# A memory-attention, ReLU² and SoLU chain: the last group's maximum taken by a matmul with ones instead of GpSimd's all-reduce, scales made ahead, and the last tile's output product done in two column halves

## The chip, the core and the metric

The kernel runs on one core of one Trainium2 chip. The metric is the device time of one execution in microseconds, from three timed runs. One further execution was recorded by the hardware profiler, and every time inside the kernel comes from that one.

The engines are named as the profile names them: PE is the matrix engine (PEld its weight loads), DVE the vector engine, ACT the scalar engine, POOL is GpSimd, and SPq and ACTq are the two queues from which the DMAs here are issued. Each engine works its instructions off in the order in which the program lists them for it, and waits for other engines by semaphores.

## The reference

Three stages follow each other. Attention over 32 memory slots per head gives `x` of 4608 tokens by 512. The second stage is a two-layer block with a squared ReLU. The third, with which this change has to do, is this:

```python
def _moe2_ref(x, w_in, w_out, g_ln):
    h = x @ w_in                                   # 4608 x 512 by 512 x 1024
    h_max = np.max(h, axis=-1, keepdims=True)
    e = np.exp(h - h_max)
    sm = e / (np.sum(e, axis=-1, keepdims=True) + 1e-09)
    solu = h * sm
    mu = np.mean(solu, axis=-1, keepdims=True)
    var = np.mean((solu - mu) ** 2, axis=-1, keepdims=True)
    ln = (solu - mu) / np.sqrt(var + 1e-06) * g_ln
    return (ln @ w_out).astype(np.float32)         # by 1024 x 512
```

All inputs and outputs are float32.

## The kernel before

**Precision.** Most products are made from float16 pairs: each factor is scaled by a power of two and split into a high and a low half, and three products (high by high, high by low, low by high) are added up in PSUM. `PASSES` lists the three. So each operand needs a scale before it can be split.

**Scales of x.** The 4608 tokens of the third stage's input fall into four groups of 1152. For each group the kernel finds the largest magnitude: every x tile leaves a column of per-partition maxima, `x_max(g)` reduces these columns on DVE, and `all_max` takes the maximum over the 128 partitions on POOL, in one all-reduce (L182). `x_scale(g)` turns the result into a scale in six tiny DVE instructions; `x_col(p)` gives the column of scales for a pair `p`, and where a pair straddles two groups it adds two more instructions to combine them (L1534).

**Third stage.** It runs over 18 pairs of 128-token tiles (`pair`, L1683). Of each pair, seven block products fill three PSUM banks on PE (`product`, L1610), ACT copies the banks out (L1701, L1709, L1720, L1736) and DVE adds to them (L1681). Then each tile goes through `solu_max`, `solu_exp`, `solu_2`, `solu_3` and `solu_4`: maximum (DVE), exponential (ACT), normalisation (DVE, and on POOL the `rstd` of L1661 and the `so` of L1662), float16 high half (ACT, L1668), low half (DVE, L1673), and a DMA transpose into `lt` (L1675). Two pairs later `gemm4` multiplies the transposed tile by `w_out` in 24 matmuls (L1760), `out4` scales the PSUM bank on ACT (L1774) and sends it to DRAM. Pair `p` also splits the x of pair `p+1` (`split_part`: ACT L1580, DVE L1582), with the scale from `x_col`.

**Order.** The program is recorded in the order in which it is written: `pair` lists the steps by hand and puts the `gemm4` pieces of an earlier pair (`fill`) between the products, so that PE has something to do while ACT and DVE work on the banks. A wait therefore holds everything written behind it for the same engine. The last group's maximum is taken after pair 1; its scale is first needed by pair 13. The scale of group 1, though, is made inside pair 3, when it splits the x of pair 4, which straddles groups 0 and 1. After pair 17 come the last four tiles' products (`rest`) with nothing else left for PE.

Of the kernel before, what the change touches and what calls it, by code (L numbers as in the profile page):

```python
# [8 lines left out]
FP32 = mybir.dt.float32  # L9
FP16 = mybir.dt.float16  # L10
# [56 lines left out]
def tile_mem_attention__moe_relu2__solu_ln(  # L67
# [15 lines left out]
    nc = tc.nc  # L83
# [136 lines left out]

    def mm_max(dg):
        w = dg.shape[1]
        mp = ps_h.tile([128, 2, 512], FP32, tag="h", name="mp")
        nc.tensor.matmul(
            out=mp[:, 0, 0:128 * w], lhsT=pools_b["ones"], rhs=dg.rearrange("p w t -> p (w t)"), start=True, stop=True
        )
        al = pools_b["m"].tile([128, w], FP32, tag=f"mal{w}", name="mal")
        nc.vector.tensor_reduce(
            out=al, in_=mp[:, 0, 0:128 * w].rearrange("p (w t) -> p w t", w=w), op=ALU.max, axis=AX
        )  # L230
        return al

# [1191 lines left out]

    def prep2_open():
        attn_ctx.close()
        for nm, bufs in (("x", 2), ("s", 2), ("o", 2)):
            pools_b[nm] = ctx.enter_context(tc.tile_pool(name=f"pb_{nm}", bufs=bufs))
        w2 = wts.tile([128, 16384], FP16, tag="win", name="w2_t")
        W2["out"] = w2[:, 0:2 * KF2 * DM].rearrange("p (a k f) -> p a k f", a=2, k=KF2)  # L1430
        W2["hi"] = w2[:, 2 * KF2 * DM:2 * KF2 * DM + 14 * 512].rearrange("p (b k f) -> p b k f", b=7, k=2)
        W2["lo"] = [raw_p.tile([128, 7, 512], FP16, tag="raw", name="w2_lo") for k in range(2)]
        for i in range(8):
            tag = ("e2", "nat", "lt", "lt")[i // 2]
            W2[i] = pools_b["s"].tile([128, 2, 512], FP32, tag=tag, name="w2", bufs=4 if tag == "lt" else 2)
# [44 lines left out]
    def prep2(i):  # L1480
        if i == 0:
            w2_sums(0)
            for k in range(2):
                w2_split(k, 0)
                w2_split(k, 1)
        elif i == 1:
            w2_split(0, 2)
            w2_split(0, 3)
            w2_sums(1)
        elif i == 2:  # L1490
            w2_split(1, 2)
            w2_split(1, 3)
            load_x(0)
            load_x(1)
        elif i == 3:
            sums_x(0)
            x_col(0)
        elif i == 5:
            split_part(0, 0)
        elif i == 7:  # L1500
            split_part(0, 1)
            load_x(2)
            sums_x(1)
# [23 lines left out]
    def x_scale(g):  # L1527
        sc = pow2_scale(xal_t.pop(g), xiv[:, g:g + 1])
        nc.vector.tensor_scalar(out=xsc[:, g:g + 1], in0=sc, scalar1=0.25, scalar2=None, op0=ALU.mult)
        nc.vector.tensor_tensor(out=xiv[:, g:g + 1], in0=xiv[:, g:g + 1], in1=iw2, op=ALU.mult)  # L1530

    xcol_t = {}

    def x_col(p):  # L1534


        g0, g1 = p * 256 // GRP, (p * 256 + 255) // GRP
        for g in (g0, g1):
# [104 lines left out]
    def solu_2(p, t):  # L1643
# [19 lines left out]
            out=so, in0=so, scalar1=mv[:, 0:1], scalar2=rstd[:, 0:1], op0=ALU.add, op1=ALU.mult  # L1663
        )

    def solu_3(p, t):
        nat = pools_b["s"].tile([128, 2, DFF2], FP16, tag="nat", name="nat")
        nc.scalar.copy(out=nat[:, 0, :], in_=h_of(p, t))  # L1668
        so_t[p, t] = nat

    def solu_4(p, t):
        nat = so_t.pop((p, t))
        nc.vector.tensor_tensor(out=nat[:, 1, :], in0=h_of(p, t), in1=nat[:, 0, :], op=ALU.subtract)  # L1673
        lt = pools_b["s"].tile([128, 2, KF2, 128], FP16, tag="lt", name="lt", bufs=4)
        nc.sync.dma_start_transpose(  # L1675
            out=lt.rearrange("p a k t -> p (a k) t"), in_=nat.rearrange("p a f -> p (a f)")
        )
        ln_t[2 * p + t] = lt
# [72 lines left out]
    out_v = out.rearrange("(b p c) d -> b c p d", b=NB, c=C)  # L1751

    def gemm4(i, part):
        if part == 0:
            gt["y4", i] = ps_y.tile([128, 512], FP32, tag="y", name="y2")
        lt, y = ln_t[i], gt["y4", i]
        steps = [(f, pl, pw) for f in range(KF2) for pl, pw in PASSES]
        for x in range(6 * part, 6 * part + 6):
            f, pl, pw = steps[x]
            nc.tensor.matmul(  # L1760
                out=y[:, 0:DM],
                lhsT=lt[:, pl, f, :],
                rhs=W2["out"][:, pw, f, :],
                start=(x == 0),
                stop=(x == len(steps) - 1),
            )
        if part == 3:
            ln_t.pop(i)

    def out4(i):  # L1770
        if i < 0:
            return
        o = pools_b["o"].tile([128, DM], FP32, tag="o", name="o")
        nc.scalar.activation(out=o, in_=gt.pop(("y4", i))[:, 0:DM], func=ACTF.Copy, scale=io2[:, 0:1])  # L1774
        for x, (off, n, bb, c, p) in enumerate(runs(i * 128, 128)):
            eng = nc.scalar if i == NTILE - 1 and x else nc.sync
            eng.dma_start(out=out_v[bb, c, p:p + n, :], in_=o[off:off + n, :])

    def tiles4(p):
        return [lambda i=i, part=part: gemm4(i, part) for i in (2 * p, 2 * p + 1) for part in range(4)]  # L1780
# [51 lines left out]
    with tc.manual_schedule():  # L1832
        make_identity(nc, ident)
        nc.vector.memset(ones, 1.0)
        nc.vector.memset(nhalf, -0.5)
        nc.vector.memset(half, 0.5)
        nc.gpsimd.memset(pmx, LOWEST)
        nc.vector.memset(c15, 2.0 ** -15)
        nc.vector.memset(kmT, 0.0)
        nc.vector.memset(ones_f, 1.0)  # L1840

        for step in FIRST.split():
            name, _, at = step.partition(".")
            now[0] = step
            STEPS[name](*(int(a) for a in at))
        now[0] = ""
        nc.gpsimd.dma_start(out=gl, in_=g_ln.rearrange("(k p) -> p k", p=128))

        LAST = NB - 1
        for n in range(1, NB):  # L1850
            for j in range(2):
                if n == 1 and j == 0:
                    w_in_scale()
                    load_q(2, 3)
                    early_load(0)
# [12 lines left out]
                if n % 2 and j and n < LAST:  # L1868
                    x_max(n // 2)
                    xal_t[n // 2] = all_max(xal_t[n // 2], "xal")  # L1870


        pair(0, [lambda d=d, x=x: gemm2_q(LAST, 1, d, x) for d in (1, 2) for x in range(4)])
        pair(1, [lambda x=x: gemm2_q(LAST, 1, 3, x) for x in range(4)], (0, 1, 1, 2))
        x_max(3)
        xal_t[3] = all_max(xal_t[3], "xal")
        for p in range(2, NPAIR):
            pair(p, tiles4(p - 2))
        p = NPAIR - 1
# [46 lines left out]
```

## Time and profile before

| | us |
|---|---|
| median of three runs | 1064.44 (1062.96 to 1064.65) |
| the profiled execution | 1064.40 |
| its span, first to last instruction | 1062.6 |
| busy on PE, of the span | 1031.9 (97%) |
| busy on DVE | 831.4 (78%) |
| busy on ACT | 579.5 (55%) |
| busy on POOL | 232.8 (22%) |

PE is busy nearly all the time, so what matters is the few places where it is not: an instruction of another engine is worth something only where PE waits for it. Matmuls overlap, so in the timeline the busy time of a row is a little more than the row's share of PE's time; the distance between the starts of two equal rows is the better measure. Between two pairs everything repeats, so one pair's period can be compared with the next one's. A row's square brackets give the idle time of its engine just before it and what ended it; "issue" there means that the profile shows nothing that the engine waited for.

### The profile page before, as it was taken

The numbers are of one execution on the slowest core, as the hardware profiler recorded it, in microseconds if no ns is written. First come the engines' busy times: TensorE is split into PE (matmuls) and PEld (weight loads), VectorE is DVE, ScalarE is ACT, GpSimd is POOL, SyncE is SP. The second block draws the span as 40 slices with busy tenths as digits, with TensorE's granted clock in tenths as the row PEclk, the third lists the DMA queues.
The fourth block names the chain that finished last, engine by engine and source line by source line (L and its number), as shares of the span: only waits on it lengthen the run. The fifth ranks groups of instructions, "written<-read, shape, count | busy, mean of one in ns | idle before, by whom it ended". The sixth has DMA issues, their size and how long they took to land.

```text
span 1062.6 us, 21249 instructions
## 1 busy us (share of the span) xinstructions
PE 1031.9 (97%) x8569; PEld 684.2 (64%) x8569; DVE 831.4 (78%) x1548; ACT 579.5 (55%) x869; POOL 232.8 (22%) x237
## 2 busy tenths in 40 slices
PE   5799999999999999999999999999799999999998
PEld 4577777777777777777777777764344444444443
DVE  4889988868768767768768766787888898898872
ACT  3689755653654554563563654753544555545442
POOL 0000200220120120120120134232343353353411
PEclk9999999999999999999999999999899999999999
DMA  9994533733832833833832343123345354354343
GB/s 290 289 271 130 128 109 89 170 104 69 200 102 76 196 99 72 201 98 79 194 97 57 63 147 114 44 60 95 90 106 119 93 128 104 86 136 103 80 90 89
DMA packets 196402, 129.25 MB, mean 122 GB/s; under 512 B 137168, under 2 KB 179408, under 8 KB 196304
## 3 DMA queue, kind: packets, MB, share of 16 engines
q1 hardware_dynamic: 196160, 127.70, 46.7%
q8 instruction: 67, 1.10, 0.5%
q14 instruction: 31, 0.25, 0.1%
q10 hardware_dynamic: 112, 0.20, 0.1%
q0 software_dynamic: 32, 0.00, 0.0%
HBM read 71.83 MB, written 23.07 MB: 89 GB/s over the span
## 4 chain that ended last, share of the span: by engine, by line
PE 87%; DVE 6%; DMA 3%; issue 2%; ACT 1%; SPq 0%; POOL 0%; ACTq 0%; DVEq 0%; POOLq 0%
PE y L1200 32%; PE hp L1118 15%; PE y L1760 15%; PE hb L1610 13%; PE y L1040 2%; PE hp L1012 2%; PE wp L736 2%; DMA q_s<-in_q_dram 2%; PE sp L885 1%; PE kp L526 1%; DMA wt_s<-in_v_dram 1%; DVE hmx L1629 1%; DMA kv_s<-in_v_dram 1%; DVE bs L1654 1%; DVE so L1649 1%
## 5 line engine op out<-in xcount | busy, mean ns | idle before, releaser
L1200 PE MATMUL y<-g,w_out 128*128 128x288 f16 x2688 | 339.6, 286 | 0.0
L1200 PEld LDWEIGHTS <-w_out 128*128 128x128 f16 x2880 | 277.3, 97 | 87.8 <-issue 12.3
L1760 PE MATMUL y<-w_t,lt 128*128 128x512 f16 x864 | 201.0, 381 | 0.5 <-DMA lt<-nat 0.5
L1610 PE MATMUL hb<-w_t,xs 128*128 128x512 f16 x504 | 165.3, 381 | 6.3 <-ACT so L1701 6.3
L1118 PE MATMUL hp<-aT,vwt 128*128 128x288 f16 x1344 | 166.9, 286 | 0.0
L1118 PEld LDWEIGHTS <-vwt 128*128 128x128 f16 x1344 | 131.4, 98 | 33.3 <-issue 0.2
L1760 PEld LDWEIGHTS <-lt 128*128 128x128 f16 x864 | 84.8, 98 | 103.6 <-issue 1.7
L1610 PEld LDWEIGHTS <-xs 128*128 128x128 f16 x756 | 74.3, 98 | 95.0 <-issue 8.4
L1610 PE MATMUL hb<-w_lo,xs 128*128 128x512 f16 x252 | 96.0, 381 | 0.0
L1183 DVE TENSOR_TENSOR g<-r_s,g 128x576 f16<-128x576 f32 x112 | 88.3, 788 | 3.9
L1222 ACT ACTIVATE x<-y,bcol,cs 128x288 f32<-128x288 f32 x60 | 35.2, 586 | 101.1 <-PE y L1200 88.4
L1176 ACT ACTIVATE r_s<-r 128x576 f32<-128x576 f32 x112 | 76.7, 685 | 21.2 <-DVE g L1183 18.2
L1129 ACT ACTIVATE r<-hp 128x576 f32<-128x576 f32 x120 | 77.4, 645 | 13.2 <-PE hp L1118 7.2
L1661 POOL TENSOR_TENSOR rstd<-ve,nhalf 128x1 f32<-128x1 f32 x36 | 35.3, 982 | 215.2 <-DVE mv L1659 208.3
L1101 DVE CAST g<-r_s 128x576 f16<-128x576 f32 x112 | 54.0, 482 | 19.1 <-ACT r_s L1176 19.1
L1668 ACT CAST nat<-so 128x1024 f16<-128x1024 f32 x36 | 37.4, 1040 | 53.9 <-POOL so L1662 53.9
L321 DVE TENSOR_REDUCE xmx<-x 128x1 f32<-128x288 f32 x64 | 28.8, 450 | 47.9 <-ACT x L1222 47.6
L1681 DVE TENSOR_TENSOR so<-hb,so 128x512 f32<-128x512 f32 x54 | 37.2, 689 | 27.4 <-PE hb L1610 27.2
L1673 DVE TENSOR_TENSOR nat<-so,nat 128x1024 f16<-128x1024 f32 x36 | 45.5, 1263 | 9.4 <-ACT nat L1668 9.2
L962 POOL TENSOR_TENSOR e<-e,ssm 96x512 f32<-96x512 f32 x18 | 18.8, 1046 | 153.8 <-DVE ssm L957 121.1
L1638 ACT ACTIVATE e<-so,nm,xiv 128x1024 f32<-128x1024 f32 x36 | 44.7, 1242 | 9.9 <-DVE nm L1631 9.9
L1662 POOL TENSOR_SCALAR so<-so,mv,rstd 128x1024 f32<-128x1024 f32 x36 | 49.0, 1361 | 3.8
(269 smaller groups left out, 1432.5 us busy)
## 6 DMA issues: line engine op xcount, KB each, us to landing
x_d<-x SPq DMA_DIRECT2D x64, 144.0 KB, 2.0
kv_s<-in_k_dram SPq DMA_DIRECT2D x31, 288.0 KB, 8.4
kv_s<-in_v_dram SPq DMA_DIRECT2D x31, 288.0 KB, 9.0
xt<-x_d SPq DMA_DIRECT2D x16, 512.0 KB, 4.3
q_s<-in_q_dram SPq DMA_DIRECT2D x21, 288.0 KB, 5.0
out_dram<-o SPq DMA_DIRECT2D x23, 192.0 KB, 2.3
w_out<-in_moe_w_in_dram SPq DMA_DIRECT2D x4, 1024.0 KB, 15.7
raw<-in_moe_w_out_dram SPq DMA_DIRECT2D x4, 1024.0 KB, 11.9
```

Source lines behind the costliest of these rows:

```text
L1101: nc.vector.tensor_copy(out=g_of(n, j, 0)[:, 2 * fp:2 * fp + 2, 0:BLK], in_=gt["r2", j, fp])
L1118: nc.tensor.matmul(out=hp[:, u, 0:BLK], lhsT=vt[:, pw, R, f * 128:(f + 1) * 128], rhs=aT[:, CJ * j:CJ * (j + 1), pa, R, :], start=(x == 0) ...
L1129: nc.scalar.activation(out=r, in_=gt.pop(("h", j, fp))[:, :, 0:BLK], func=ACTF.Relu, scale=scale)
L1176: nc.scalar.activation(out=r2, in_=r, func=ACTF.Square)
L1183: (nc.vector if eng == "D" else nc.gpsimd).tensor_tensor(out=g_of(n, j, 1)[:, fs, 0:BLK], in0=gt.pop(("r2", j, fp)), in1=g_of(n, j, 0)[:, ...
L1200: nc.tensor.matmul(out=y[:, 0:w], lhsT=w_out_t[d][:, pw, f, :], rhs=g_of(n, j, pg)[:, f, 0:w], start=(x == 0), stop=(x == len(steps) - 1),)
L1610: nc.tensor.matmul(out=hp_t[p][bank], lhsT=xs[:, px, a, kk, :], rhs=W2["lo"][kk][:, b, :] if pw else W2["hi"][:, b, kk, :], start=first an ...
L1638: nc.scalar.activation(out=e, in_=h_of(p, t), func=ACTF.Exp, scale=iv[:, 0:1], bias=nm[:, 0:1], accum_out=sm)
L1662: nc.gpsimd.tensor_scalar(out=so, in0=so, scalar1=mv[:, 0:1], scalar2=rstd[:, 0:1], op0=ALU.add, op1=ALU.mult)
L1668: nc.scalar.copy(out=nat[:, 0, :], in_=h_of(p, t))
L1673: nc.vector.tensor_tensor(out=nat[:, 1, :], in0=h_of(p, t), in1=nat[:, 0, :], op=ALU.subtract)
L1760: nc.tensor.matmul(out=y[:, 0:DM], lhsT=lt[:, pl, f, :], rhs=W2["out"][:, pw, f, :], start=(x == 0), stop=(x == len(steps) - 1),)
```

## The change

1. The maximum of the last group (group 3) is taken otherwise. `mm_max_put` puts the per-partition maxima on the diagonal of a 128 by 128 tile (one DVE instruction, after pair 1); at the head of pair 4 `mm_max` multiplies it by a tile of ones on PE into a PSUM bank of the tag `h2`, and DVE reduces the bank. The tile of ones is set by POOL when the third stage's pools are opened. The three earlier groups keep the all-reduce.
2. `x_col` remembers its results, and the columns of pairs 0, 4, 5 and 9 are made together at the time when only that of pair 0 was made; the column of pair 13 is made right after `mm_max`.
3. At the end, `solu_3` and `solu_4` of tile 34 are written before `solu_2` of tile 35; those of tile 35 stand two pieces of `rest` later than before, behind `out4` of tile 32; tile 35's transpose is issued in two parts, high half and low half.
4. Tile 35's product runs in two halves of 256 columns, 24 matmuls each, the high-half passes first in each; `out4` evicts and stores each half by itself.

```diff
     def mm_max(dg):
         w = dg.shape[1]
-        mp = ps_h.tile([128, 2, 512], FP32, tag="h", name="mp")
+        mp = pools_b["h"].tile([128, 512], FP32, tag="h2", name="mp")
...
+        pools_b["ones"] = pools_b["m"].tile([128, 128], FP32, tag="ones", name="ones_m")
+        nc.gpsimd.memset(pools_b["ones"], 1.0)
...
             sums_x(0)
-            x_col(0)
+            for p in (0, 4, 5, 9):
+                x_col(p)
...
+    def solu_T(p, t, a):
+        nat, lt = so_t[p, t], ln_t[2 * p + t]
+        nc.sync.dma_start_transpose(
+            out=lt[:, a].rearrange("p a k t -> p (a k) t"), in_=nat[:, a].rearrange("p a f -> p (a f)")
+        )
...
         lt, y = ln_t[i], gt["y4", i]
-        steps = [(f, pl, pw) for f in range(KF2) for pl, pw in PASSES]
-        for x in range(6 * part, 6 * part + 6):
-            f, pl, pw = steps[x]
+        w = DM // halves
+        order = [(f, ps) for f in range(KF2) for ps in PASSES]
+        if i == NTILE - 1:
+            order.sort(key=lambda s: s[1][0])
+        steps = [(h, f, pl, pw) for h in range(halves) for f, (pl, pw) in order]
+        for h, f, pl, pw in steps[6 * halves * part:6 * halves * (part + 1)]:
             nc.tensor.matmul(
-                out=y[:, 0:DM],
+                out=y[:, h * w:(h + 1) * w],
                 lhsT=lt[:, pl, f, :],
-                rhs=W2["out"][:, pw, f, :],
...
         x_max(3)
-        xal_t[3] = all_max(xal_t[3], "xal")
+        xal_t[3] = mm_max_put(xal_t[3])
         for p in range(2, NPAIR):
+            if p == 4:
+                xal_t[3] = mm_max(xal_t[3])
+                x_col(13)
             pair(p, tiles4(p - 2))
...
         solu_max(p, 1)
         out4(2 * p - 3)
+        solu_3(p, 0)
         solu_exp(p, 1)
+        solu_4(p, 0)
         solu_2(p, 1)
-        solu_3(p, 0)
-        solu_4(p, 0)
         for x, f in enumerate(rest):
             f()
-            if x == 2:
+            if x == 4:
                 solu_3(p, 1)
                 solu_4(p, 1)
-            if x % 4 == 3:
+            if x == 13:
+                out4(2 * p + 1, 0)
+            elif x == 15:
+                out4(2 * p + 1, 1)
+            elif x % 4 == 3:
                 out4(2 * p - 2 + x // 4)
```

On POOL, at the end of pair 1 and in pair 2, the kernel before has these rows (`al` is the all-reduced maximum, `rstd` and `so` the two steps of the normalisation; L1661 and L1662 are lines before the change):

```order
L1662 TENSOR_SCALAR so<-so,mv,rstd 128x1024
L184 ISA
L184 ISA al<-xmax 128x1
L1661 ISA
L1661 TENSOR_TENSOR rstd<-ve,nhalf 128x1
L1662 TENSOR_SCALAR so<-so,mv,rstd 128x1024
```

and the changed kernel, at the same place, these:

```order
L1667 TENSOR_SCALAR so<-so,mv,rstd 128x1024
L1666 TENSOR_TENSOR rstd<-ve,nhalf 128x1
L1667 TENSOR_SCALAR so<-so,mv,rstd 128x1024
L1568 TENSOR_TENSOR xm<-xt 128x256
L1568 TENSOR_TENSOR xm<-xm,xt 128x256
```

The all-reduce is gone, and with it an ISA row ahead of it and another ahead of the `rstd` that follows.

On DVE, inside pair 3, the kernel before makes the scale of group 1 between the maximum `hmx` of a tile and the split `xs` of pair 4:

```order
L1631 TENSOR_SCALAR nm<-hmx,xiv 128x1
L238 TENSOR_SCALAR pm_9449<-al 128x1
L240 TENSOR_SCALAR ex<-pm_9449 128x1
L244 TENSOR_SCALAR sc<-ex 128x1
L247 TENSOR_SCALAR xiv<-ex 128x1
L1529 TENSOR_SCALAR xsc<-sc 128x1
L1530 TENSOR_TENSOR xiv<-xiv,iw_112 128x1
L1545 TENSOR_TENSOR xsc<-xsc 128x1
L1545 TENSOR_TENSOR xiv<-xiv 128x1
L1582 SCALAR_TENSOR_TENSOR xs<-xm,xsc,xs 128x1024
```

In the changed kernel that place has no such rows, and the head of pair 4 has these on DVE, with the reduction of PE's bank `mp` first:

```order
L1664 TENSOR_SCALAR mv<-mv 128x1
L228 TENSOR_REDUCE mal<-mp 128x1
L238 TENSOR_SCALAR pm_9631<-mal 128x1
L240 TENSOR_SCALAR ex<-pm_9631 128x1
L244 TENSOR_SCALAR sc<-ex 128x1
L247 TENSOR_SCALAR xiv<-ex 128x1
L1532 TENSOR_SCALAR xsc<-sc 128x1
L1533 TENSOR_TENSOR xiv<-xiv,iw_112 128x1
L1550 TENSOR_TENSOR xsc<-xsc 128x1
L1550 TENSOR_TENSOR xiv<-xiv 128x1
L1634 TENSOR_REDUCE hmx<-so 128x1
```

So the eight scale instructions leave the stretch in front of pair 4's split and stand, for another group, in front of a `hmx` one pair later.

On PE, in the changed kernel, the two halves of the last tile meet here (`y` is the PSUM bank, `lt` the transposed tile, `w_t` holds w_out; the wait is for ACT):

```order
L1779 LDWEIGHTS lt
L1779 MATMUL y_12236<-w_t,lt 128x256
L1779 LDWEIGHTS lt
L1779 MATMUL y_12236<-w_t,lt 128x256 [waits Activation_49]
L1779 LDWEIGHTS lt
L1779 MATMUL y_12236<-w_t,lt 128x256
```

The fourth row is the second half's first matmul: it waits until ACT has evicted the first half. The kernel before has 24 matmuls of 512 columns there and no wait among them.

## Rows read from the trace of the kernel before

**Rows 1.** Waits of PE over the span: who for whom, total, times, longest.

```profile
PE hb L1610 <- ACT so L1701: 6.3, 1, 6.3
...
PE y L1760 <- DMA lt<-nat: 0.5, 1, 0.5
```

**Rows 2.** Busy time by stretch: length, PE, PEld, DVE, ACT, POOL, PE clock.

```profile
750.00:760.00 10.00, 10.00 (x38) 4.11 (x37) 9.27 (x17) 5.99 (x11) 5.73 (x6) 0.78 0.46 104
```

**Rows 3.** Timeline of all engines, pairs 2 and 3: start, busy, engine, line.

```profile
720.66 2.75 PE L1760 MATMUL y<-w_t,lt 128*128 128x512 f16 x12
...
728.29 0.56 POOL L184 PARTITION_ALL_REDUCE al<-xmax  x1 [6.07 <-DVE mv L1659]
...
735.73 0.59 POOL L1661 TENSOR_TENSOR rstd<-ve,nhalf 128x1 f32<-128x1 f32 x1 [6.88 <-issue]
...
738.74 1.47 DVE L1673 TENSOR_TENSOR nat<-so,nat 128x1024 f16<-128x1024 f32 x1 [6.37 <-ACT nat L1668]
...
740.08 2.75 PE L1760 MATMUL y<-w_t,lt 128*128 128x512 f16 x12
...
745.93 0.14 DVE L238 TENSOR_SCALAR pm<-al 128x1 f32<-128x1 f32 x1
...
746.74 0.15 DVE L1545 TENSOR_TENSOR xiv<-xiv 128x1 f32<-128x1 f32 x1
746.92 1.15 ACT L1580 ACTIVATE xs<-xm,xsc 128x1024 f16<-128x1024 f32 x1 [5.93 <-DVE xiv L1545]
...
748.54 0.57 ACT L1701 COPY so<-hb 128x512 f32<-128x512 f32 x1
...
749.17 0.59 PE L1610 MATMUL hb<-w_t,xs 128*128 128x512 f16 x1 [6.33 <-ACT so L1701]
```

**Rows 4.** Timeline of all engines in pair 5, an undisturbed one.

```profile
788.01 2.75 PE L1760 MATMUL y<-w_t,lt 128*128 128x512 f16 x12
...
788.33 0.58 ACT L1709 COPY so<-hb 128x512 f32<-128x512 f32 x1
...
793.19 0.38 PE L1610 MATMUL hb<-w_t,xs 128*128 128x512 f16 x1
```

**Rows 5.** Timeline of DVE after the scale of group 0.

```profile
664.02 0.45 DVE L321 TENSOR_REDUCE xmx<-x 128x1 f32<-128x288 f32 x1 [4.49 <-ACT x L1222]
```

**Rows 6.** Timeline of POOL where the third stage's pools are opened.

```profile
632.91 1.76 POOL L1460 TENSOR_TENSOR w2s<-w 128x512 f32<-128x512 f32 x1 [8.97 <-DMA w<-w_d]
```

**Rows 7.** Line L204, six ones-by-diagonal products: ns min/median/max, first and last start.

```profile
L204 PEld LDWEIGHTS mp<-first x12: 186/191/338, 21.3 to 121.4; 128*128 128x128 f32 x12
L204 PE MATMUL mp<-first x12: 272/275/579, 21.3 to 121.5; 128*128 128x128 f32 x12
```

**Rows 8.** Line L209, the reduction of such a bank.

```profile
L209 DVE TENSOR_REDUCE first<-mp x6: 277/282/292, 28.0 to 122.0; 128x1 f32<-128x128 f32 x6
```

**Rows 9.** Line L173, nine float16 matmuls of 256 columns in a row.

```profile
L173 PE MATMUL ta<-first x9: 272/273/283, 42.7 to 43.6; 128*128 128x256 f16 x9
```

**Rows 10.** Timeline of all engines at the end.

```profile
1035.36 11.82 PE L1760 MATMUL y<-w_t,lt 128*128 128x512 f16 x54
...
1042.71 1.22 DVE L1673 TENSOR_TENSOR nat<-so,nat 128x1024 f16<-128x1024 f32 x1
...
1047.66 10.53 PE L1760 MATMUL y<-w_t,lt 128*128 128x512 f16 x48 [0.49 <-DMA lt<-nat]
...
1058.29 0.69 ACT L1774 ACTIVATE o<-y,io 128x512 f32<-128x512 f32 x1 [4.49 <-PE y L1760]
1059.00 0.39 ACTq L1777 DMA_DIRECT2D out_dram<-o  x1
```

**Rows 11.** Groups of ACT by shape: busy, mean ns of one.

```profile
L1580 ACT ACTIVATE xs<-xt,xsc 128x256 f16<-128x256 f32 x18 | 9.0, 500 | 0.0
```

**Rows 12.** DMA issues in the last 33 us: KB, median us to landing.

```profile
out_dram<-o SPq DMA_DIRECT2D x4, 64.0 KB, 2.2
out_dram<-o ACTq DMA_DIRECT2D x1, 192.0 KB, 2.6
```

More of the change, by code (lines that the diff above doesn't have):

```diff
@@ L222, in mm_max @@
         w = dg.shape[1]
-        mp = ps_h.tile([128, 2, 512], FP32, tag="h", name="mp")
+        mp = pools_b["h"].tile([128, 512], FP32, tag="h2", name="mp")
         nc.tensor.matmul(
-            out=mp[:, 0, 0:128 * w], lhsT=pools_b["ones"], rhs=dg.rearrange("p w t -> p (w t)"), start=True, stop=True
+            out=mp[:, 0:128 * w], lhsT=pools_b["ones"], rhs=dg.rearrange("p w t -> p (w t)"), start=True, stop=True
         )
@@ L228, in mm_max @@
         nc.vector.tensor_reduce(
-            out=al, in_=mp[:, 0, 0:128 * w].rearrange("p (w t) -> p w t", w=w), op=ALU.max, axis=AX
+            out=al, in_=mp[:, 0:128 * w].rearrange("p (w t) -> p w t", w=w), op=ALU.max, axis=AX
         )
@@ L1426, in prep2_open @@
         attn_ctx.close()
-        for nm, bufs in (("x", 2), ("s", 2), ("o", 2)):
+        for nm, bufs in (("x", 2), ("s", 2), ("o", 2), ("m", 1)):
             pools_b[nm] = ctx.enter_context(tc.tile_pool(name=f"pb_{nm}", bufs=bufs))
@@ L1530, in x_scale @@
         nc.vector.tensor_tensor(out=xiv[:, g:g + 1], in0=xiv[:, g:g + 1], in1=iw2, op=ALU.mult)
-    xcol_t = {}
+    col_t = {}
     def x_col(p):
+        if p in col_t:
+            return col_t[p]
         g0, g1 = p * 256 // GRP, (p * 256 + 255) // GRP
@@ L1540, in x_col @@
                 x_scale(g)
+        c = col_t[p] = g0 if g0 == g1 else NT // GRP + g0 // 2
         if g0 == g1:
-            return g0
-        c = NT // GRP + g0 // 2
+            return c
         for t, op in ((xsc, ALU.min), (xiv, ALU.max)):
@@ L1669, in solu_3 @@
         so_t[p, t] = nat
+        if 2 * p + t == NTILE - 1:
+            ln_t[2 * p + t] = pools_b["s"].tile([128, 2, KF2, 128], FP16, tag="lt", name="lt", bufs=4)
+            solu_T(p, t, slice(0, 1))
     def solu_4(p, t):
-        nat = so_t.pop((p, t))
+        nat = so_t[p, t]
         nc.vector.tensor_tensor(out=nat[:, 1, :], in0=h_of(p, t), in1=nat[:, 0, :], op=ALU.subtract)
[L1674 to L1678, printed above, removed]
+        if 2 * p + t == NTILE - 1:
+            solu_T(p, t, slice(1, 2))
+        else:
+            ln_t[2 * p + t] = pools_b["s"].tile([128, 2, KF2, 128], FP16, tag="lt", name="lt", bufs=4)
+            solu_T(p, t, slice(0, 2))
+        so_t.pop((p, t))
     def h_add(out_, bank):
@@ L1753, in gemm4 @@
     def gemm4(i, part):
+        halves = 2 if i == NTILE - 1 else 1
         if part == 0:
@@ L1756, in gemm4 @@
         lt, y = ln_t[i], gt["y4", i]
-        steps = [(f, pl, pw) for f in range(KF2) for pl, pw in PASSES]
-        for x in range(6 * part, 6 * part + 6):
-            f, pl, pw = steps[x]
+        w = DM // halves
[4 more added lines that the diff above has]
+        for h, f, pl, pw in steps[6 * halves * part:6 * halves * (part + 1)]:
             nc.tensor.matmul(
-                out=y[:, 0:DM],
+                out=y[:, h * w:(h + 1) * w],
                 lhsT=lt[:, pl, f, :],
-                rhs=W2["out"][:, pw, f, :],
-                start=(x == 0),
-                stop=(x == len(steps) - 1),
+                rhs=W2["out"][:, pw, f, h * w:(h + 1) * w],
+                start=(f == 0 and (pl, pw) == PASSES[0]),
+                stop=(f == KF2 - 1 and (pl, pw) == PASSES[-1]),
             )
@@ L1768, in gemm4, with out4 @@
             ln_t.pop(i)
-    def out4(i):
+    def out4(i, half=None):
         if i < 0:
             return
-        o = pools_b["o"].tile([128, DM], FP32, tag="o", name="o")
-        nc.scalar.activation(out=o, in_=gt.pop(("y4", i))[:, 0:DM], func=ACTF.Copy, scale=io2[:, 0:1])
+        cs = slice(0, DM) if half is None else slice(half * DM // 2, (half + 1) * DM // 2)
+        if not half:
+            gt["o", i] = pools_b["o"].tile([128, DM], FP32, tag="o", name="o")
+        o = gt["o", i]
+        nc.scalar.activation(out=o[:, cs], in_=gt["y4", i][:, cs], func=ACTF.Copy, scale=io2[:, 0:1])
         for x, (off, n, bb, c, p) in enumerate(runs(i * 128, 128)):
-            eng = nc.scalar if i == NTILE - 1 and x else nc.sync
-            eng.dma_start(out=out_v[bb, c, p:p + n, :], in_=o[off:off + n, :])
+            eng = nc.scalar if half and x else nc.sync
+            eng.dma_start(out=out_v[bb, c, p:p + n, cs], in_=o[off:off + n, cs])
     def tiles4(p):
```

## The prediction

> **What bounds the kernel now.** I read the waits of PE first, since PE is the engine that is nearly always busy. From the third stage on there are two entries: one wait of 6.3 us for ACT's copy L1701, and one of 0.5 us for a transpose [rows 1]. The reader is to see that nothing else holds PE there, so the change can be worth something at two places only. The second view is the timeline around the long wait. PE's twelve `gemm4` matmuls at the head of a pair start at 720.66 in pair 2 and at 740.08 in pair 3, a period of 19.42 us [rows 3]. In pair 5 they start at 788.01 [rows 4]. Two periods would have taken 38.84 us; 47.93 us went by, so the long wait costs 788.01 − 740.08 − 38.84 = 9.09 us. That is more than 6.33 us: in the stretch after it PE's granted clock averages 0.78 [rows 2], that is, part of it at 1.2 GHz and the rest at 2.4 GHz, after PE had stood idle. So about 2.8 us of the 9.09 are matmuls at half pace.
>
> Read backwards, the wait is a chain [rows 3]. PE starts at 749.17, when ACT's copy (748.54 plus 0.57) is done. ACT is in order, and ahead of the copy stands the split `xs` of pair 4, held for 5.93 us by the last of eight scale instructions on DVE. DVE is in order too, and had been held for 6.37 us by an ACT cast, which needs `so` from POOL. POOL's `rstd` started at 735.73 after 6.88 us in which it waited for nothing shown; before that gap stands the all-reduce (728.29, itself 0.56 us). Its input, `mv`, was done by then: the all-reduce's own row names it as the last event before it. That label is odd, since the all-reduce reads `xmax` and not `mv`; the 6.07 us ahead of it may be a gap of the same kind, and the change takes both away.
>
> **The change, part by part.**
>
> *The maximum of group 3.* With the all-reduce and its two ISA rows gone, POOL can go from `mv` to `rstd` at once. DVE then does not wait 6.37 us, and the eight scale instructions (745.93 to 746.74 plus 0.15, 0.96 us [rows 3]) no longer stand in pair 3. Together 6.37 + 0.96 = 7.33 us: the copy L1701, which ended at 749.11, ends at 741.78 or earlier. PE, whose twelve matmuls from 740.08 take 12 × 0.216 us (19.42 us hold 90 of them, 48 for `gemm4` and 42 products), comes to it at 742.67. That is 0.9 us to spare, and this is the worst case, since ACT's split of pair 4 needs nothing from DVE any more. What is late next is nothing on PE: I take the whole 9.09 us, the half-pace matmuls with it. Were the copy late after all by up to a microsecond, that would be the loss; a 0.49 us wait at the end left its 48 matmuls at 10.53 us, full pace [rows 10].
>
> What is added. On PE one float32 product of ones by a diagonal, in order between two pairs, so it can only cost. The trace has six like it, two passes each: 191 ns of weight load and 275 ns of matmul per pass [rows 7]. Between 0.22 us (two matmuls at the 0.11 us that 128 float32 columns would take if twice a float16 row's 256 columns, rows 9) and 0.93 us (everything in series); I take 0.40 us, two weight loads, the row that sets the pace when a load is longer than a matmul. Its operands are no wait: the diagonal is written 35 us earlier. The diagonal costs DVE about 0.28 us, as the reduction does [rows 8], where PE has those 0.9 us. At the head of pair 4 DVE now has the reduction and eight small instructions ahead of `hmx`, 0.28 + 0.96 us, and waits for PE's product behind the last fill, up to a microsecond: some 2.2 us later. Behind `hmx` hang `nm`, ACT's exponential, a cast and the copy L1709. In pair 5 that copy ends at 788.91 and the product that needs its bank starts at 793.19 [rows 4]: 4.3 us of cover against 2.2. Cost nothing.
>
> *Scales made ahead.* Fourteen more small DVE instructions (0.12 us each by the 0.96 for eight, 1.7 us) behind the scale of group 0. DVE idles 4.49 us there, until an ACT eviction [rows 5]. Nothing; without that cover 1.7 us of DVE's time. The memset of ones on POOL stands in front of subtractions that wait 8.97 us for their DMA [rows 6]: nothing.
>
> *The end, tile 34.* Its low half is written at 1042.71 on DVE and the transpose holds PE at 1047.66 [rows 10]. Ahead of `solu_2` of tile 35 it does not wait for that step's passes over 1024 columns, two at the least, of which this row's pass shows the length: 1.22 us. So the transpose starts over 2 us earlier and the wait goes. The 0.49 us are counted from a modelled end; against 0.216 us a matmul PE lost 0.65 us (the 54 from 1035.36 should be followed at 1047.01). Gain 0.65. Tile 35's exponential stands behind one ACT cast more, up to 1.2 us by a pass of that width; but its low half is wanted only after 16 short matmuls, 1.8 us into the tile. Nothing; without that cover up to 1.2 us.
>
> *The end, halves.* 48 matmuls of 256 columns: nine of them start between 42.7 and 43.6 us, 0.9 / 8 = 0.11 us apart, each 0.273 long to its last result [rows 9]; 48 × 0.11 = 5.28 us against 24 × 0.216 = 5.18: cost 0.10. The first matmul of the second half waits for the eviction of the first, as the order shows. That gap is 0.16 us (0.273 − 0.11, the last result coming out), 0.10 us to ACT's start (1058.19 to 1058.29), the eviction, and 0.06 us back (749.11 to 749.17). For 256 columns the nearest row is 0.50 us [rows 11], so 0.82 us; from 0.7 (half of 0.69) to 1.0 (the full 0.69). The last eviction is shorter by 0.19. The last DMA from ACT is 96 KB instead of 192: by 2.6 us for 192 and 2.2 for 64 [rows 12] some 0.3 us shorter; between 0 and 0.4. The halving thus costs 0.10 + 0.82 − 0.19 − 0.30 = 0.43 us by itself; with the 0.65, the end gains 0.22, between a gain of 0.5 and a loss of 0.3.
>
> On the gap: the order has the matmul wait for a read of other columns of the same bank. The Trainium skill (PSUM — Partial Sum Buffer, "PSUM bank collisions raise a hardware error") says to guard PSUM by bank and not by address, since TensorE's writes and ScalarE's reads of one bank must not overlap. By that rule the gap stays whatever the columns, and speaks against halving in one bank; without the wait the end would gain 0.82 us more.
>
> On the DMA: the Trainium skill (DMA: Bandwidth & Descriptors, "Anatomy of one DMA — SWDGE (gpsimd) path") gives a fixed part of about 2.0 us and the bytes at 436 GB/s for another queue. By it 96 KB fewer are an estimated 0.22 us instead of 0.30, and the sum 0.08 us longer.
>
> **Sum.** The profiled execution took 1064.40 us, 1.8 more than its span and 0.04 less than the median of the three runs, so I add to it directly: 1064.40 − 9.09 + 0.40 − 0.22 = 1055.5 us.
>
> **Rivals.**
>
> *PE stops a second time.* DVE now carries the reduction ahead of `hmx` in pair 4, and it had been behind through pairs 0 to 2. If it still is when pair 4 begins, its 2.2 us fall on top; past the 4.3 us of cover PE waits for L1709. Against it: DVE idled 6.37 us in pair 2, and pair 5 shows the cover. With 1 to 4 us lost again, half pace included: 1057 to 1060, say 1058.
>
> *The gap on POOL is not the all-reduce's.* The profile names no cause for the 6.88 us. Then DVE's wait stays, and only the 0.96 us of scale instructions go, which leaves the wait near 5.4 us and the half pace: 1064.4 − 1.0 + 0.4 − 0.2 = 1063.6. Against it: the gap stands right between the two ISA rows, and the `rstd` of the other pairs starts with its input.
>
> *Slower: the memset holds POOL.* The tile of ones lies in space that the attention leaves, so the memset waits for its last users; behind it stand POOL's subtractions, behind these the splits of the third stage's weights on ACT and DVE, and behind those the last ReLU work of the second stage, which PE needs. The first 8.97 us of such a wait are free [rows 6]; after that each microsecond is PE's, and from about 18 us on (8.97 + 8.9) the kernel is slower than before. At 21 us it would take 1067.6. For it: in-order queues. Against it: by the order the users are an old matmul and two transposes, all listed behind the attention's own work, and the subtractions' DMAs need the same space.
>
> **Chances.** Forecast 0.81 (own range 1053.8 to 1057.2); a second stop 0.13 (1057 to 1060); the gap stays 0.04; slower 0.02. The three runs of before lie 1.7 us apart, which is the lower margin: 1053.8. Upwards I go to 1059.0, into most of the second stop. About 0.2%, 2.1 us, is what a measurement of this kernel can tell from no change: faster 0.94, same 0.04, slower 0.02.
>
> **What would show it.** Right: in the new trace the `gemm4` heads of pairs 3, 4 and 5 are 19.4 us apart (19.8 once, for the product); POOL's `rstd` in pair 2 begins with its input; PE's waits have no L1701; a gap of 0.8 us on PE in the middle of tile 35, and none ahead of tile 34. Wrong: a PE wait of over a microsecond in pairs 3 or 4, a granted clock under 1 near 750, or a PE wait around 640.

## The result, and the profile after

| | before | after |
|---|---|---|
| median | 1063.88 us (4 runs, 1062.96 to 1064.65) | 1054.92 us (4 runs, 1053.95 to 1056.60) |
| the profiled execution | 1064.40 us | 1054.11 us |
| its span | 1062.6 us | 1052.3 us |
| head of pair 2 to head of pair 4 (`gemm4` on PE) | 47.93 us | 39.07 us |
| head of pair 4 to the end of the span | 294.01 us | 293.39 us |

The head of a pair is the start of its twelve `gemm4` matmuls. The profile gives the span to a tenth of a microsecond, so the last row is good to 0.05 us. The four runs of before are the three known before the change and one more.

The ratio is 0.9918, 95% interval 0.9900 to 0.9935: faster by some 9 us, where 8.9 were predicted. A second measurement of the changed kernel gave 1054.86 us, ratio 0.9908 (0.9891 to 0.9925).

The waits of PE from the third stage on (who for whom, total, times, longest), to set against [rows 1]:

```profile
PE y L1779 <- ACT o L1796: 0.6, 1, 0.6
```

The long wait for the copy and the one for the transpose are gone; a new one stands in the last tile. The two stretches that held the long wait and the half-pace matmuls (columns as in [rows 2]: busy us of PE, PEld, DVE, ACT, POOL, then granted clock, DMA share, GB/s):

```profile
740.00:750.00 10.00, 10.00 (x48) 4.48 (x47) 9.48 (x18) 5.49 (x9) 5.80 (x6) 1.00 0.37 84
750.00:760.00 10.00, 10.00 (x49) 4.72 (x48) 8.54 (x26) 4.85 (x8) 2.77 (x3) 1.00 0.54 128
```

PE is busy throughout at a granted clock of 1.00, where it was 0.78 in the second stretch. The timeline of the changed kernel, from the head of pair 2 into pair 3, against [rows 3] (L1666 and L1667 are the old L1661 and L1662, L1716 the old L1701):

```profile
719.84 2.75 PE L1779 MATMUL y<-w_t,lt 128*128 128x512 f16 x12
...
726.71 1.51 POOL L1666 TENSOR_TENSOR rstd<-ve,nhalf 128x1 f32<-128x1 f32 x1 [5.31 <-DVE mv L1664]
728.32 1.53 POOL L1667 TENSOR_SCALAR so<-so,mv,rstd 128x1024 f32<-128x1024 f32 x1
729.89 1.04 ACT L1679 CAST nat<-so 128x1024 f16<-128x1024 f32 x1 [4.25 <-POOL so L1667]
...
731.49 1.64 DVE L1687 TENSOR_TENSOR nat<-so,nat 128x1024 f16<-128x1024 f32 x1
...
734.76 1.15 ACT L1585 ACTIVATE xs<-xm,xsc 128x1024 f16<-128x1024 f32 x1
736.92 0.59 ACT L1716 COPY so<-hb 128x512 f32<-128x512 f32 x1 [0.43 <-PE hb L1615]
739.26 2.75 PE L1779 MATMUL y<-w_t,lt 128*128 128x512 f16 x12
```

POOL's `rstd` begins when `mv` is there, 6.87 us after the head of the pair instead of 15.07. DVE's low half `nat` has no idle time in front of it, the split `xs` waits for nothing, and the copy is done at 737.51, before PE has even begun the twelve matmuls behind which it needs it. In pair 4, the product of ones by the diagonal (`mp`), its reduction, and what follows:

```profile
754.80 0.38 PE L224 MATMUL mp<-dg,ones_m 128*128 128x128 f32 x2
755.02 0.38 PE L1615 MATMUL hb<-w_t,xs 128*128 128x512 f16 x1
755.22 0.29 DVE L228 TENSOR_REDUCE mal<-mp 128x1 f32<-128x128 f32 x1 [1.05 <-PE mp L224]
...
756.45 1.21 DVE L1634 TENSOR_REDUCE hmx<-so 128x1 f32<-128x1024 f32 x1
...
758.91 2.75 PE L1779 MATMUL y<-w_t,lt 128*128 128x512 f16 x12
...
760.18 0.57 ACT L1724 COPY so<-hb 128x512 f32<-128x512 f32 x1
```

The next product starts 0.22 us behind `mp`: that is its whole price. The copy ends at 760.75; PE wants it 5.18 us after the head of the pair (793.19 − 788.01 in [rows 4]), at 764.09. The end, against [rows 10]:

```profile
1025.68 19.62 PE L1779 MATMUL y<-w_t,lt 128*128 128x512 f16 x102
1029.10 1.23 DVE L1687 TENSOR_TENSOR nat<-so,nat 128x1024 f16<-128x1024 f32 x1 [1.14 <-ACT nat L1679]
...
1045.38 0.47 ACT L1796 ACTIVATE o<-y,io 128x256 f32<-128x256 f32 x1 [1.93 <-PE y L1779]
1045.91 2.78 PE L1779 MATMUL y<-w_t,lt 128*128 128x256 f16 x24 [0.61 <-ACT o L1796]
1048.72 0.47 ACT L1796 ACTIVATE o<-y,io 128x256 f32<-128x256 f32 x1 [2.87 <-PE y L1779]
1049.23 0.39 ACTq L1799 DMA_DIRECT2D out_dram<-o  x1
```

The 102 matmuls run without a stop: 78 of 512 columns at 0.216 us and 24 of 256 at 0.109 (2.78 less the 0.273 of the last one, over 23). They would be followed at 1045.15, and are at 1045.91.

**Where the 10.3 us of span went.** 0.82 before pair 2 (719.84 against 720.66): the kernels differ by as much in the first 40 us, on DMA waits that the change does not touch, and the profiles of the changed kernel and its variants have that head between 718.7 and 721.1. 8.86 from pair 2 to pair 4. 0.62 from there to the end. Since the first piece moves by more than a microsecond from execution to execution, small differences below are read from the two stretches of the table and not from medians.

### The profile page after: what moved, and what is told of

Its sections match the earlier page's. It is cut to its first block, busy times and chain, and to the rows that moved or that the text cites. A ratio compares the mean times of both kernels' runs of the same rounds, so it can differ in the third digit from the quotient of the medians.

```text
span 1052.3 us, 21305 instructions
## 1 busy us (share of the span) xinstructions
PE 1030.0 (98%) x8595; PEld 686.2 (65%) x8595; DVE 827.5 (79%) x1550; ACT 580.2 (55%) x870; POOL 230.3 (22%) x237
## 4 chain that ended last, share of the span: by engine, by line
PE 96%; DMA 2%; DVE 1%; SPq 0%; ACT 0%; issue 0%; ACTq 0%
PE y L1200 34%; PE y L1779 18%; PE hp L1118 16%; PE hb L1615 16%; PE hp L1012 3%; PE y L1040 3%; PE wp L736 2%; DMA q_s<-in_q_dram 2%; PE sp L885 1%; PE kp L526 1%; DMA wt_s<-in_v_dram 1%; PE wp L694 1%; PE kp L566 1%; PE tq L646 1%; SPq L385 0%; PE kp L540 0%
## 5 line engine op out<-in xcount | busy, mean ns | idle before, releaser
L1779 PE MATMUL y<-w_t,lt 128*128 128x512 f16 (+1 forms) x888 | 199.7, 373 | 0.6 <-ACT o L1796 0.6
L1666 POOL TENSOR_TENSOR rstd<-ve,nhalf 128x1 f32<-128x1 f32 x36 | 36.3, 1007 | 214.6 <-DVE mv L1664 214.6
L1667 POOL TENSOR_SCALAR so<-so,mv,rstd 128x1024 f32<-128x1024 f32 x36 | 48.5, 1348 | 3.8
```

The costliest lines, as they stand in the source:

```text
L1667: nc.gpsimd.tensor_scalar(out=so, in0=so, scalar1=mv[:, 0:1], scalar2=rstd[:, 0:1], op0=ALU.add, op1=ALU.mult)
L1779: nc.tensor.matmul(out=y[:, h * w:(h + 1) * w], lhsT=lt[:, pl, f, :], rhs=W2["out"][:, pw, f, h * w:(h + 1) * w], start=(f == 0 and (pl, p ...
```

## The experiments

Theory: the all-reduce itself, standing in pair 2, made POOL late, and everything else in pairs 2 to 4 followed from it. Rivals: the scale instructions in pair 3 are an equal part of the cost; POOL's gap is not the all-reduce's; the end contributes. Each kernel below was timed against the kernel before:

| run | median (range, runs), us | ratio, 95% | heads 2 to 4 | head 4 to end |
|---|---|---|---|---|
| e1_scales_late | 1056.01 (1055.06 to 1056.45, 4) | 0.9924 (0.9908 to 0.9939) | 39.07 | 293.42 |
| e2_allreduce_scales_ahead | 1060.33 (1059.89 to 1060.35, 5) | 0.9964 (0.9951 to 0.9977) | 44.63 | 293.42 |
| e3_end_only | 1064.08 (1062.76 to 1065.53, 10) | 0.9999 (0.9988 to 1.0009) | 48.87 | 293.47 |
| e7_warm | 1062.13 (1060.85 to 1063.37, 10) | 0.9982 (0.9973 to 0.9992) | 45.80 | 294.08 |
| e6_second_allreduce | 1055.38 (one run) | | 39.07 | 293.46 |
| e9_place_only | 1055.14 (1054.53 to 1058.83, 6) | 0.9924 (0.9906 to 0.9942) | 38.85 | 294.11 |
| e5_no_halves | 1054.86 (1054.40 to 1055.20, 4) | 0.9905 (0.9892 to 0.9919) | 39.06 | 293.34 |
| e4_two_banks | 1053.67 (1053.40 to 1055.92, 4) | 0.9899 (0.9883 to 0.9915) | 39.07 | 292.65 |
| e8_place_two_banks | 1053.48 (1052.65 to 1056.02, 5) | 0.9901 (0.9884 to 0.9917) | 38.85 | 292.67 |

### Scales made late again: e1_scales_late

The changed kernel, with only the scale of pair 0 made early:

```diff
-            for p in (0, 4, 5, 9):
-                x_col(p)
+            x_col(0)
```

> The changed kernel, but the scales of pairs 4, 5 and 9 are made where they were before; the matmul maximum and the end stay changed. Theory (the all-reduce held DVE 6.4 us through POOL, the eight scale instructions are under 1 us of the rest): the copy that PE waits for comes at most 0.3 us late, PE's wait in pair 3 is 0 to 0.5 us, and the time is that of the changed kernel, 1055 us, within 0.6. Rival (the scales standing in the split's way were the larger part): PE waits 2 us or more in pair 3, its clock falls, 1058 to 1060.

The heads are 39.07 us apart as in the changed kernel: making the scales ahead saves no time once the all-reduce is gone. What it adds is room. The head of pair 3 and the copy, in e1's timeline:

```profile
740.24 2.75 PE L1778 MATMUL y<-w_t,lt 128*128 128x512 f16 x12
...
741.74 0.57 ACT L1715 COPY so<-hb 128x512 f32<-128x512 f32 x1
```

The copy ends at 742.31 and PE comes to it at 742.83, twelve matmuls behind the head: 0.5 us to spare, against 4.3 us (737.51 and 741.85) with the scales made ahead.

### The all-reduce put back: e2_allreduce_scales_ahead

```diff
-        xal_t[3] = mm_max_put(xal_t[3])
+        xal_t[3] = all_max(xal_t[3], "xal")
         for p in range(2, NPAIR):
-            if p == 4:
-                xal_t[3] = mm_max(xal_t[3])
-                x_col(13)
```

> The changed kernel, but with the all-reduce on POOL for the last group; scales ahead and the end stay changed. Two readings of the chain. By the prediction's second rival, DVE's 6.4 us wait stays and the copy L1716 comes 1 us earlier only: a wait of 5.4 us on PE, half pace after it, 1063.3. By the timeline followed further: ACT's split no longer needs DVE and starts at 741.0, the copy ends at 743.3 and costs PE 0.7 us, then the copy L1724 stands behind the exponential, whose maximum DVE delivers at 746.0, ends at 749.1 and costs PE 3.1 us: together 3.9 us in two waits, 1055 + 3.9 - 0.2 = 1058.7, up to 1060.5 if the clock falls. POOL's gap before the rstd stays near 6.9 us by both.

5.8 us more than 38.85 go by between the heads. Its timeline:

```profile
727.60 0.83 POOL L184 PARTITION_ALL_REDUCE al<-xmax  x1 [5.80 <-DVE mv L1664]
735.78 0.59 POOL L1666 TENSOR_TENSOR rstd<-ve,nhalf 128x1 f32<-128x1 f32 x1 [7.36 <-issue]
...
743.82 0.38 PE L1615 MATMUL hb<-w_t,xs 128*128 128x512 f16 x1 [1.39 <-ACT so L1716]
...
748.95 0.38 PE L1615 MATMUL hb<-w_t,xs 128*128 128x512 f16 x1 [2.39 <-ACT so L1724]
```

POOL is as late as before, and PE stops twice instead of once. The waits are 3.78 us; the granted clock in the stretches from 740 and 750 is 0.97 and 0.86, and matmuls at half pace, 0.43 us apart near 750.6 instead of 0.216, are the other 2.0. So the scales ahead save 3.3 us on the heads while the all-reduce stays (44.63 against 47.93; 4.2 against the 48.87 of e3 below, which differs from e2 in the scales alone), and nothing when it goes: the two parts of the change treat the same stall, and their gains do not add up.

### The end alone: e3_end_only

The kernel before with the changes 3 and 4 of the list alone: the all-reduce at its old place (as in e2's diff) and the scales late (as in e1's). The tile of ones is still set, but nothing reads it.

> Of the change only the end is left (tile 34 first, tile 35 in halves); all-reduce and late scales as before. Theory: PE's 6.3 us wait and the half pace after it are back, pairs 3 to 5 take 47.9 us between their heads; the end is 0.6 us shorter than before, as in the trace of the changed kernel: 1063.3. Rival (the end hides nothing and gains more, or nothing): 1062 or 1064.

The end takes 293.47 us, 0.54 less than before, and the time cannot be told from no change. The wait in pair 3 is there again, in its list of PE's waits:

```profile
PE hb L1614 <- ACT so L1715: 6.9, 1, 6.9
```

It is 0.6 us longer than in the kernel before, with the same order of instructions there: so much can such a stop vary between two profiles.

### The half pace by itself: e7_warm

The kernel before, with 24 matmuls of 512 columns, whose result nobody reads, where PE would stand idle:

```diff
+        if p == 3:
+            warm = pools_b["h"].tile([128, 512], FP32, tag="h2", name="warm")
+            for _ in range(24):
+                nc.tensor.matmul(
+                    out=warm, lhsT=W2["out"][:, 0, 0, 0:128], rhs=W2["out"][:, 0, 0, :], start=True, stop=True
+                )
         product(p, 6)
```

> The kernel before with 24 matmuls more of 512 columns on PE, into a bank that nobody reads, written where PE stands idle in pair 3: 24 x 0.216 = 5.2 us inside the 6.3 us wait. Theory (2.8 of the 9.1 us are half pace after idling): the granted clock stays 1.0, pair 3 to pair 5 takes 45.2 us instead of 47.9, 1061.2. Rival (the 2.8 us are not the clock's but late banks): no gain, 1063.9; if the matmuls overrun the wait, slower.

Its wait, the added matmuls, and its stretch after the wait (columns as above):

```profile
PE hb L1610 <- ACT so L1701: 1.6, 1, 1.6
```

```profile
741.23 5.34 PE L1720 MATMUL warm<-w_t 128*128 128x512 f16 x24
```

```profile
750.00:760.00 10.00, 10.00 (x48) 4.50 (x46) 9.76 (x17) 5.08 (x9) 6.78 (x6) 1.00 0.47 121
```

The clock stays at 1.00. Of the 6.95 us lost between the heads, 24 × 0.216 = 5.18 are the added matmuls and 1.56 the wait, and only 0.2 remain, where the kernel before has 2.8. Useless matmuls in the idle time gave back 2.1 us. The half pace was a cost of the stop.

### An all-reduce elsewhere: e6_second_allreduce

The changed kernel with one all-reduce more, of a value that nobody needs, at the head of pair 8:

```diff
         for p in range(2, NPAIR):
+            if p == 8:
+                all_max(iw2, "dum")
```

> The changed kernel with one all-reduce of 128 x 1 on POOL at the head of pair 8, whose result nobody uses. Theory (the all-reduce makes POOL stand still before and after it): about 6 us without work before it and 6.9 us behind it, on POOL alone, and the rstd that follows about 8 us late; PE loses 0 to 1 us, since the cover of an undisturbed pair is just enough. Rival (the gap in the kernel before had another cause): POOL loses the 0.6 us of the instruction and nothing else.

Its timeline, from pair 7 to the head of pair 9:

```profile
821.70 1.51 POOL L1666 TENSOR_TENSOR rstd<-ve,nhalf 128x1 f32<-128x1 f32 x1 [6.15 <-DVE mv L1664]
...
833.77 1.19 POOL L1667 TENSOR_SCALAR so<-so,mv,rstd 128x1024 f32<-128x1024 f32 x1
840.71 0.38 POOL L184 PARTITION_ALL_REDUCE al<-iw  x1 [5.74 <-issue]
...
840.95 0.14 DVE L1664 TENSOR_SCALAR mv<-mv 128x1 f32<-128x1 f32 x1
...
848.64 0.59 POOL L1666 TENSOR_TENSOR rstd<-ve,nhalf 128x1 f32<-128x1 f32 x1 [7.55 <-DVE so L1696]
...
856.04 0.57 ACT L1716 COPY so<-hb 128x512 f32<-128x512 f32 x1
...
857.27 2.75 PE L1779 MATMUL y<-w_t,lt 128*128 128x512 f16 x12
```

The operand was there before pair 0, where the first scale of x is made with it, so nothing in the program holds POOL for 5.74 us before the all-reduce; the standstill comes with the operation, and the prediction's reading of the 6.07 us holds. The `rstd` behind it names DVE's `so`, which it does not read; its input `mv` was there at 841.09.

The trace shows what stands at the start of both gaps. Where the order has an ISA row, the trace has a pair of records named `MODIFY_POOL_CONFIG`, in e6 at 835.16 to 835.21 and at 841.04 to 841.16, and POOL starts nothing for 5.50 us behind the first pair and 7.48 us behind the second; in pair 2 of the kernel before it is 5.83 and 6.80. So the time goes with POOL's turn from other work to the all-reduce and back. Where POOL's neighbouring instructions are copies or other all-reduces, no such pair stands between them, and there is no gap, as here in the attention of the kernel before:

```profile
348.10 0.63 POOL L470 COPY pmx<-pm 64x128 f32<-64x128 f32 x2 [15.29 <-DVE pm L418]
348.83 1.09 POOL L471 PARTITION_ALL_REDUCE pm<-pmx  x1
349.99 0.29 POOL L474 COPY pm<-pm 64x128 f32<-64x128 f32 x1
```

In e6 the next `rstd` starts 7.5 us late (a period of 19.42 us would put it at 841.12). Yet PE waits for nothing in pairs 8 and 9. The rows suggest why: `rstd` starts 3.28 us behind the head of pair 7 (818.42), but 6.87 us behind the head of pair 2 in the changed kernel, so DVE has made up 3.6 us by then and the delay falls into that room. The copy ends at 856.61, 3.2 us before PE wants it (859.86, twelve matmuls behind the head at 857.27).

### One line moved: e9_place_only

If the operation is free in pair 8, the kernel before needs only this:

```diff
-        xal_t[3] = all_max(xal_t[3], "xal")
         for p in range(2, NPAIR):
+            if p == 8:
+                xal_t[3] = all_max(xal_t[3], "xal")
             pair(p, tiles4(p - 2))
```

> The kernel before with one line moved: the all-reduce of group 3 stands at the head of pair 8 instead of pair 2; scales as late as before, old end. Theory (the place of the all-reduce was the cost): no PE wait in pairs 2 to 4; the span from the PE head of pair 2 to that of pair 4 is 38.9 us instead of 47.9, nothing is lost in pair 8, and the time is 1063.9 - 9.1 = 1054.8 us plus or minus 1.5. Rival (before pair 4 DVE and POOL have no slack, and the scale instructions in pair 3 alone still make PE wait): part of the 9 us stays, 1057 to 1061. Second rival (at pair 8, with the all-reduce's standstill on POOL, the late scales and the old end, PE waits there instead): 39 us between the heads of pairs 2 and 4, but a PE wait of some microseconds in pair 8 or 9.

The theory holds: 38.85 us between the heads, all of the 9.1. Its timeline in pair 3 and pair 8:

```profile
739.26 2.75 PE L1760 MATMUL y<-w_t,lt 128*128 128x512 f16 x12
...
740.74 0.57 ACT L1701 COPY so<-hb 128x512 f32<-128x512 f32 x1
...
839.45 0.38 POOL L184 PARTITION_ALL_REDUCE al<-xmax  x1 [5.94 <-issue]
846.61 0.59 POOL L1661 TENSOR_TENSOR rstd<-ve,nhalf 128x1 f32<-128x1 f32 x1 [6.79 <-DVE so L1681]
```

POOL stands still around the all-reduce as ever, and PE's only wait is the 0.5 us for the transpose at the end. The copy ends at 741.31, 0.5 us before PE needs it, as in e1. Two of its six executions took 1057.6 and 1058.8 us; their mean granted clock was 0.998 and 0.996, where the other four have 1.00 and the kernel before, with its stop, 0.994 to 0.996. That points to a stop of PE in them, but neither was profiled, and where it stood stays open.

### The halves: e5_no_halves and e4_two_banks

e5 is the changed kernel with the last tile's product in one piece. The tile keeps the new order of its passes, its transpose in two parts and its place:

```diff
-        halves = 2 if i == NTILE - 1 else 1
+        halves = 1
...
-            if x == 13:
-                out4(2 * p + 1, 0)
-            elif x == 15:
-                out4(2 * p + 1, 1)
-            elif x % 4 == 3:
+            if x % 4 == 3:
```

> The changed kernel with the last tile in one piece: 24 matmuls of 512 columns, one eviction, two DMAs of 64 and 192 KB; the tile order and the two-part transpose stay. By the prediction the halving costs 0.4 us: 0.4 us faster than the changed kernel. By the trace of the changed kernel the halving costs 0.06 for the short matmuls and 0.76 for the gap and gives back 0.22 on the eviction and 0.53 behind the last DMA's issue: no difference, within 0.2 us between the last tile's start and the span's end.

e4 is the changed kernel with the second half's product in a PSUM bank of its own:

```diff
+        if halves == 2 and part == 2:
+            gt["z4", i] = pools_b["h"].tile([128, 512], FP32, tag="h0", name="z2")
...
-                out=y[:, h * w:(h + 1) * w],
+                out=ys[h][:, h * w:(h + 1) * w],
...
-        nc.scalar.activation(out=o[:, cs], in_=gt["y4", i][:, cs], func=ACTF.Copy, scale=io2[:, 0:1])
+        nc.scalar.activation(out=o[:, cs], in_=gt["z4" if half else "y4", i][:, cs], func=ACTF.Copy, scale=io2[:, 0:1])
```

> The changed kernel with the second half of the last tile in a PSUM bank of its own, so that its first matmul waits for no eviction. Theory (the gap is the wait for the shared bank): the 0.76 us gap on PE in the middle of tile 35 is gone, the end after pair 5 takes 273.2 us instead of 274.0, the time is 0.7 us less than the changed kernel's. Rival (the gap has another cause, or the first half's eviction and DMAs now delay the second's): gap or end unchanged.

> The changed kernel once more, as the measure for the two kernels beside it: 1054.9 us, between 1053.9 and 1056.6.

The last eviction and the last DMA issue of e5, then the second half of e4 (`z` is the second bank), in their timelines:

```profile
1048.20 0.69 ACT L1796 ACTIVATE o<-y,io 128x512 f32<-128x512 f32 x1 [4.49 <-PE y L1779]
1048.92 0.39 ACTq L1799 DMA_DIRECT2D out_dram<-o  x1
```

```profile
1045.18 2.78 PE L1781 MATMUL z<-w_t,lt 128*128 128x256 f16 x24
1045.43 0.47 ACT L1798 ACTIVATE o<-y,io 128x256 f32<-128x256 f32 x1 [1.93 <-PE y L1781]
1048.00 0.47 ACT L1798 ACTIVATE o<-z,io 128x256 f32<-128x256 f32 x1 [2.10 <-PE z L1781]
```

In one piece the end takes 293.34 us, in halves 293.39 to 293.47: halving in one bank gains nothing. In e4 the second half follows without a gap, while ACT evicts the first, and the end takes 292.65, 0.74 to 0.82 less. By the times alone (1053.67 and 1054.86, ranges that overlap) this could not be told; in the trace it can.

### Both lessons together: e8_place_two_banks

e4, and in it:

```diff
-        xal_t[3] = mm_max_put(xal_t[3])
         for p in range(2, NPAIR):
-            if p == 4:
-                xal_t[3] = mm_max(xal_t[3])
-                x_col(13)
+            if p == 8:
+                xal_t[3] = all_max(xal_t[3], "xal")
```

> The changed kernel, with the second column half of the last tile in a PSUM bank of its own, and the maximum over partitions of group 3 by the all-reduce at the head of pair 8 instead of by the matmul with ones at the head of pair 4; the scales of groups 0 to 2 made ahead. Theory: 38.84 us from the PE head of pair 2 to that of pair 4 and no float32 product behind it, no wait of PE in pairs 8 and 9; 0.22 us less on PE than with the product, and from the head of pair 4 to the end of the span 292.4 to 292.7 us; time 1053.4 us plus or minus 1.5, which beats both kernels by trace, though 0.2 us less than the two-bank version alone cannot be told from its time. Rival (the all-reduce costs PE something there, being needed by pair 13): a PE wait between pairs 8 and 13 and over 293 us from the head of pair 4 to the end.

38.85 us between the heads, no wait of PE in the third stage, and 292.67 us to the end: the product's 0.22 us saved beside e4, and nothing paid in pair 8. At 1053.48 us it has the lowest median measured. It is 1.4 us below the changed kernel, of which the traces account for 0.22 + 0.75 = 1.0; the times alone would not separate it from e4.

## Why the prediction was right

- *The wait of 6.33 us and the half pace behind it, 9.09 us.* Right in mechanism and in size. The heads of pairs 2, 3 and 4 are 19.42 and 19.65 us apart; with no product (e8) the two periods take 38.85, where 38.84 were reckoned. That the 6.07 us ahead of the all-reduce belong to it was inferred from an odd label; e6 shows it. That 2.8 us were half pace: e7 leaves 0.2.
- *The 0.9 us to spare.* This was called the worst case, and it was: the margin is 4.3 us, since with the scales made ahead ACT's split waits for nothing. The sum behind it, DVE's 6.37 us and the 0.96 us of scales, was too small. By it the copy would be 0.06 us late if the scales stayed in pair 3; in e1 and e9, where they do, it has 0.5 us to spare. From before to e1 the copy's end moves from 9.03 to 2.07 us behind the head of pair 3, so the all-reduce alone was worth 6.96 us there.
- *The product on PE.* 0.40 us taken, between 0.22 and 0.93; it took 0.22, the lower end. The row chosen, two weight loads in series, was the wrong one: the two loads, 190 ns each, ran from 754.59 to 755.00 beside the matmuls in front of them, so only the two passes of 0.11 us counted.
- *DVE in pair 4 some 2.2 us later.* `hmx` starts at 756.45, in e8, which has neither reduction nor scales there, at 754.37: 2.1 us. The copy L1724, the old L1709, is 1.1 us later (760.18 against 759.05) and still 3.3 us early. Nothing, as predicted.
- *Scales ahead, memset.* Nothing, as predicted. But "nothing" holds because the all-reduce goes as well: with it in place they are worth 3.3 us.
- *The end, a gain of 0.22 us.* It was 0.62. The stop ahead of tile 34 went (0.65). Of the halving, reckoned at a cost of 0.43: matmuls +0.05 (0.10 reckoned), gap +0.76 (0.82), eviction −0.22 (−0.19), and from the last issue to the end of the span 3.07 us instead of 3.6, −0.53 where −0.30 was reckoned. That is the mis-sized term. The 96 KB landed in 2.0 us and the 192 KB in 2.6, both on ACT's queue; the row used for a smaller transfer, 2.2 us for 64 KB, was of SP's queue. That row was no measure of the size: the same queue lands 96 KB in 1.8 us and 64 KB in 1.9 in the changed kernel, and why it took longer before is not shown. The halving thus cost 0.06 us, and e5 confirms it.
- *The two rules.* The Trainium skill (PSUM — Partial Sum Buffer, "PSUM bank collisions raise a hardware error") tells to guard by bank, and by it the gap stays in one bank; the trace agrees, 0.76 us in one bank and none in two, worth 0.75 us where 0.82 was given. The wait is one that the program lists (`[waits Activation_49]` in the order); whether the chip would need it, no run here tests. By the Trainium skill (DMA: Bandwidth & Descriptors, "Anatomy of one DMA — SWDGE (gpsimd) path") 96 KB fewer were an estimated 0.22 us; the measured 0.53 decides.
- *The rivals.* No second stop came. The rival in which POOL's gap stays was priced at 1063.6 us, and this is where the working failed: e2, in which POOL's gap and the scales made ahead stand together, took 1060.33. The price counted only the 0.96 us of scale instructions, although the same text says that ACT's split of pair 4 then needs nothing from DVE; that frees the copy by more (743.19 against 748.54), until the next copy stops PE. The memset did not hold POOL.

Two errors of 0.2 and 0.4 us had one direction: by trace the change is worth 8.86 + 0.62 = 9.48 us, 1054.9 against the 1055.5 predicted.

## What to carry to other kernels

When one operation stalls a chain, ask first whether it can stand elsewhere: moving one line by six pairs, to where DVE had made up its lateness, gave the same 9 us as replacing the operation. Which is the first pair that is free, and how firmly, was not run. Parts of a change that shorten the same stall must be priced together, since either alone can look worth 3 us or nothing, and what the second one buys may be margin rather than time. Splitting the last tile so that ACT evicts one half while PE makes the other paid here only with the halves in different PSUM banks.

## What the runs showed of the hardware

- An all-reduce over partitions of one column per partition, put between other work, costs POOL far more than its row: 0.4 to 0.9 us in the row, 5.7 to 6.1 us of standstill before it and 6.8 to 7.6 us after it, in the third stage of seven kernels ([rows 3], e2, e3, e6, e7, e8, e9). Each standstill begins at a pair of `MODIFY_POOL_CONFIG` records. Between a copy and an all-reduce, or two all-reduces in a row, there is no pair and at most 0.1 us (348.10 to 349.99 and 590.45 to 591.49 in the kernel before).
- A float32 product of 128 by 128 with 128 columns, in the middle of a float16 stream, costs PE 0.22 us.
- After its stops in pair 3 PE's granted clock averaged 0.78 (before) and 0.86 (e2) over ten microseconds; after idle time filled with matmuls it was 1.00 (e7).
